# Decode attention with a gated MLP: wq as the moving operand of the query projection, and head selection by a mask on VectorE

## The chip, the cores and the metric

The kernel runs on one core of one Trainium2 chip. The metric is the device time of one execution in microseconds (us). A core has a tensor engine (PE; its weight loads are listed as PEld), a vector engine (DVE), a scalar engine (ACT), POOL, and SP, which here issues the loads. Sixteen DMA engines serve the core.

## The reference, cut to what matters

```python
# B=2 sequences, one new token each; H=32 heads, Sk=16384 cached keys, Dh=128, D=1024, bf16
q      = (x @ wq).reshape(B, 1, H, Dh)                       # wq: 1024 x 4096, 8 MB
scores = einsum(q, k_cache) * Dh**-0.5                       # k_cache: 268 MB
o      = einsum(softmax(scores), v_cache)                    # v_cache: 268 MB
a      = o.reshape(B, 1, H * Dh) @ wo                        # wo: 8 MB
# b = a small MLP of x with w1 .. w4 (19 MB);  result = g * a + (1 - g) * b
```

Every cached byte is used once. The inputs are 572.5 MB.

## The kernel before

The caches are read as 32 tiles (one sequence and two heads each) of 8 MB of K and 8 MB of V. Three buffers of 8 MB rotate: a load is issued when the buffer that it takes has been used up. For each tile, DVE transposes K in 16 pieces, PE multiplies the pieces with the query (`S`), a softmax follows, and PE multiplies with V.

The query projection takes wq as the stationary operand, so that every matmul loads 128x128 weights in order to multiply two columns:

```python
        qps = misc_psum([P, H, B])
        for h in range(H):
            for r in range(KC):
                nc.tensor.matmul(qps[:, h, :], lhsT=wq[:, r, h * Dh : (h + 1) * Dh],
                                 rhs=xT[:, r, :], start=(r == 0), stop=(r == KC - 1))
        nc.vector.tensor_copy(out=qT[:], in_=qps[:])
        # ... 8 matmuls with a 0/1 matrix selv arrange q as the K stage needs it (qsel)
```

The PV product `O` is 128 rows by 4x128 columns, of which each row has one useful quarter. ACT copies all of it to SBUF, and four fp32 matmuls with 0/1 matrices pick the quarters:

```python
        Os = ppool.tile([P, 4, Dh], FP32, tag="PrOs", name="Os")
        nc.scalar.copy(out=Os[:].rearrange("p x d -> p (x d)"), in_=O[:])
        for x in range(4):
            nc.tensor.matmul(oc[:], lhsT=Os[:, x, :], rhs=osel[:, x, :],
                             start=(x == 0), stop=(x == 3))
```

## Time and profile before

| | before |
|---|---|
| median of 6 runs | 1337.32 us (1337.11 to 1337.46) |
| bytes moved, mean rate | 573.34 MB, 429 GB/s |
| DMA queue's packets, share of 16 engines' time | 99.2% |
| PE, DVE, ACT busy | 62%, 53%, 3% |

These lines are from the page of the profile: busy time of each engine (with its share of the span and its instructions), the DMA row of the 40 slices (9 is 90% or more), and the DMA queues (packets, MB, share of 16 engines' span).

```profile
PE 830.0 (62%) x5415; PEld 381.4 (29%) x5415; DVE 709.2 (53%) x863; ACT 45.5 (3%) x100; POOL 14.3 (1%) x45
...
DMA  9999999999999999999999999999999999999997
...
q1 hardware_dynamic: 12664, 572.54, 99.2%
q8 instruction: 42, 0.69, 0.2%
q14 instruction: 14, 0.11, 0.0%
```

DMA is at 9 in every slice but the last. No engine comes near it. The queue q1 carries the kernel's loads. The queues q8 and q14 carry its own instructions.

The costliest groups show busy time and the mean ns of one instruction, then the idle time before them and what ended most of it.

```profile
L308 PE MATMUL S<-T,z 128*128 128x512 bf16 x2048 | 594.0, 423 | 324.7 <-DVE T L300 309.7
...
L300 DVE STREAM_TRANSPOSE T<-Kn 128x1024 f32<-128x1024 f32 x512 | 611.8, 1229 | 264.1 <-DMA Kn<-in_A_k_cache_dram 215.8
...
L360 ACT COPY Os<-O 128x512 f32<-128x512 f32 x32 | 18.7, 585 | 1067.2 <-PE O L352 1067.2
L362 PE MATMUL misc<-osel,Os 128*128 128x2 f32 x256 | 34.5, 257 | 22.2 <-ACT Os L360 22.2
...
L251 PE MATMUL misc<-xT,wt 128*128 128x2 bf16 x256 | 7.1, 165 | 23.3 <-DVE xT L246 20.4
```

DVE's transposes cost 1229 ns each, and 215.8 us of their 264.1 us of idle time end when a K load lands: DVE waits for DMA. The parts that the change touches are L251 (the projection, 7.1 us busy), L360 (the ACT copies, 18.7 us) and L362 (the selection, 34.5 us).

The next lines are the timeline's (start, duration, engine, line, operation), first from the start of the kernel and then around the end of one tile.

```profile
0.74 0.39 SPq L118 DMA_DIRECT2D wt<-in_A_wq_dram  x1
...
23.00 5.98 PE L251 MATMUL misc<-xT,wt 128*128 128x2 bf16 x219 [20.42 <-DVE xT L246]
...
33.04 0.33 SPq L107 DMA_DIRECT2D Vn<-in_A_v_cache_dram  x1
...
33.76 0.29 DVE L269 CAST qsel<-misc 128x128 bf16<-128x128 f32 x1 [0.49 <-PE misc L262]
...
43.63 2.37 DVE L300 STREAM_TRANSPOSE T<-Kn 128x1024 f32<-128x1024 f32 x2 [8.90 <-DMA Kn<-in_A_k_cache_dram]
```

The projection ends at 33.0 us and the query is ready (L269) at 34.05 us, but K0 lands only at 43.6 us. The V load issued at 33.04 us joins a queue with two K loads of 19.3 us each ahead of it, the first of them under way.

```profile
90.60 0.33 SPq L107 DMA_DIRECT2D Vn<-in_A_v_cache_dram  x1
...
91.62 3.68 PE L352 MATMUL O<-Vn,PT 128*32 128x512 bf16 x64
...
95.34 0.33 SPq L96 DMA_DIRECT2D Kn<-in_A_k_cache_dram  x1
95.35 0.58 ACT L360 COPY Os<-O 128x512 f32<-128x512 f32 x1 [26.99 <-PE O L352]
...
95.99 1.05 PE L362 MATMUL misc<-osel,Os 128*128 128x2 f32 x8 [0.69 <-ACT Os L360]
97.08 0.22 DVE L379 SCALAR_TENSOR_TENSOR OT<-misc,g_bc,rinv 128x2 bf16<-128x2 f32 x1 [4.66 <-PE misc L362]
```

The last PV matmul ends at 95.3 us and OT (L379) is written at 97.3 us. The buffer of V is released at the PV matmuls' end, as SP's issue of the next K at 95.34 us shows. The selection comes after that release.

### The profile page before, as it was taken

To read this page: it belongs to the slowest core of one execution; us is meant where nothing else is said; L and a number is where in the kernel's file an instruction comes from. 1 tells how busy PE (TensorE), PEld (TensorE's weight loads), DVE (VectorE), ACT (ScalarE), POOL (GpSimd) and SP (SyncE) were. 2 spreads that over 40 slices of the span, in tenths; PEclk is the share of its full clock that TensorE was granted. 3 is DMA by queue.
4 is the path that set the end of the run, shared out by engine and by line. 5 is a ranking of instruction groups with operands and counts; after the bars stand their busy time and mean duration, and the time that the engine had idled before them with its cause. 6 is when DMAs were issued, how large, how long until landed. Compare 5 with 4: busy or idle time off the path is not lost.

```text
span 1335.5 us, 12650 instructions
## 1 busy us (share of the span) xinstructions
PE 830.0 (62%) x5415; PEld 381.4 (29%) x5415; DVE 709.2 (53%) x863; ACT 45.5 (3%) x100; POOL 14.3 (1%) x45
## 2 busy tenths in 40 slices
PE   2577665677657755555766555577656557765564
PEld 2233222433225322222322222233222223222232
DVE  0666565366651665545666545566655456665530
ACT  0000000000000000000000000000000000000000
POOL 0000000000000000000000000000000000000000
PEclk9988777688776877778887777888777788877775
DMA  9999999999999999999999999999999999999997
GB/s 409 436 437 433 424 440 424 439 437 428 432 434 439 435 426 429 438 432 438 436 433 430 424 440 437 430 433 433 436 440 430 427 432 434 438 435 436 429 419 308
DMA packets 12728, 573.34 MB, mean 429 GB/s; under 512 B 1784, under 2 KB 1792, under 8 KB 2560
## 3 DMA queue, kind: packets, MB, share of 16 engines
q1 hardware_dynamic: 12664, 572.54, 99.2%
q8 instruction: 42, 0.69, 0.2%
q14 instruction: 14, 0.11, 0.0%
q10 hardware_dynamic: 8, 0.00, 0.0%
HBM read 572.53 MB, written 0.00 MB: 429 GB/s over the span
## 4 chain that ended last, share of the span: by engine, by line
PE 27%; DVE 24%; DMA 19%; another core or an unknown queue 14%; issue 13%; ACT 3%; SPq 0%; ACTq 0%; POOL 0%
DVE T L300 20%; PE S L308 14%; DMA Kn<-in_A_k_cache_dram 13%; PE O L352 7%; DMA Vn<-in_A_v_cache_dram 3%; DMA wo<-in_A_wo_dram 3%; PE misc L213 2%; PE misc L362 2%; PE misc L487 2%; ACT Pr L336 1%; DVE PT L340 1%; ACT Os L360 1%; DVE mx L329 1%; DVE mdiag L322 1%
## 5 line engine op out<-in xcount | busy, mean ns | idle before, releaser
L308 PE MATMUL S<-T,z 128*128 128x512 bf16 x2048 | 594.0, 423 | 324.7 <-DVE T L300 309.7
L300 DVE STREAM_TRANSPOSE T<-Kn 128x1024 f32<-128x1024 f32 x512 | 611.8, 1229 | 264.1 <-DMA Kn<-in_A_k_cache_dram 215.8
L308 PEld LDWEIGHTS <-z 128*128 128x128 bf16 x2048 | 217.7, 106 | 695.4 <-issue 532.1
L352 PE MATMUL O<-Vn,PT 128*32 128x512 bf16 x2048 | 121.4, 390 | 5.0 <-DMA Vn<-in_A_v_cache_dram 5.0
L379 DVE SCALAR_TENSOR_TENSOR OT<-misc,g_bc,rinv 128x2 bf16<-128x2 f32 x32 | 7.0, 220 | 159.3 <-PE misc L362 159.3
L352 PEld LDWEIGHTS <-PT 128*32 128x32 bf16 x2048 | 74.1, 140 | 51.1 <-issue 22.2
L213 PE MATMUL misc<-rs,ones_f 128*128 128x2 f32 x64 | 17.9, 349 | 79.1 <-DVE rs L372 79.1
L360 ACT COPY Os<-O 128x512 f32<-128x512 f32 x32 | 18.7, 585 | 1067.2 <-PE O L352 1067.2
L362 PE MATMUL misc<-osel,Os 128*128 128x2 f32 x256 | 34.5, 257 | 22.2 <-ACT Os L360 22.2
L362 PEld LDWEIGHTS misc<-osel,Os 128*128 128x128 f32 x256 | 31.8, 195 | 37.1 <-ACT Os L360 37.1
L319 DVE TENSOR_REDUCE m<-S 128x1 f32<-128x512 f32 x32 | 22.2, 692 | 36.9 <-PE S L308 36.9
L213 PEld LDWEIGHTS misc<-rs,ones_f 128*128 128x128 f32 x64 | 16.1, 313 | 83.9 <-issue 81.2
L340 DVE STREAM_TRANSPOSE PT<-Pr 128x512 bf16<-128x512 bf16 x32 | 22.7, 711 | 28.7 <-ACT Pr L336 28.7
L336 ACT ACTIVATE Pr<-S,nb 128x512 bf16<-128x512 f32 x32 | 22.0, 687 | 125.0 <-DVE nb L331 122.0
L213 PE MATMUL misc<-mdiag,ones_f 128*128 128x128 f32 x64 | 15.6, 326 | 16.9 <-DVE mdiag L322 16.9
L487 PEld LDWEIGHTS <-wt 128*128 128x128 bf16 x352 | 22.3, 167 | 9.8 <-DMA wt<-in_B_w_dram 8.5
L329 DVE TENSOR_REDUCE mx<-misc 64x1 f32<-64x64 f32 x64 | 14.2, 222 | 18.9 <-PE misc L213 18.5
L276 POOL TENSOR_TENSOR z<-qsel,own 128x32 bf16<-128x32 bf16 x32 | 10.6, 332 | 1205.3 <-PE S L308 1173.9
L251 PE MATMUL misc<-xT,wt 128*128 128x2 bf16 x256 | 7.1, 165 | 23.3 <-DVE xT L246 20.4
L487 PE MATMUL misc<-xn2T,wt 128*128 128x2 bf16 x224 | 14.4, 202 | 8.3 <-DMA wt<-in_B_w_dram 8.3
L376 DVE RECIPROCAL rinv<-misc 128x2 f32<-128x2 f32 x32 | 5.5, 171 | 22.7 <-PE misc L213 22.7
L576 DVE CAST rows<-out_acc 128x256 bf16<-128x256 f32 x1 | 0.4, 425 | 29.9 <-PE out_acc L393 29.9
(78 smaller groups left out, 100.0 us busy)
## 6 DMA issues: line engine op xcount, KB each, us to landing
Vn<-in_A_v_cache_dram SPq DMA_DIRECT2D x2, 4096.0 KB, 47.4
wt<-in_B_w_dram SPq DMA_DIRECT2D x1, 7168.0 KB
w<-in_B_w_dram SPq DMA_DIRECT2D x4, 1792.0 KB, 33.0
wo<-in_A_wo_dram SPq DMA_DIRECT2D x6, 1024.0 KB, 34.4
wt<-in_B_w_dram SPq DMA_DIRECT2D x2, 2048.0 KB, 37.3
wo<-in_A_wo_dram SPq DMA_DIRECT2D x2, 512.0 KB, 18.6
wo<-in_A_wo_dram SPq DMA_DIRECT2D x4, 256.0 KB, 12.7
Kn<-in_A_k_cache_dram SPq DMA_DIRECT2D x32, 51.9
```

Source lines behind the costliest of these rows:

```text
L213: nc.tensor.matmul(ps[:], lhsT=ones_f[:], rhs=src, start=True, stop=True)
L300: nc.vector.transpose(out=T[:].rearrange("p w j s -> p j w s"), in_=Kw[:, m * CW : (m + 1) * CW].rearrange("p (j w e) -> p j w e", w=2, e=32),
L308: nc.tensor.matmul(S[:], lhsT=z[:, v, NM - 1 - m : NM - 1 - m + P], rhs=Tb[:, v // 2, :, v % 2], start=(m == 0 and v == 0), stop=(m == NM ...
L319: nc.vector.reduce_max(out=m[:], in_=S[:], axis=AX.X)
L322: nc.vector.tensor_scalar(out=mdiag[:], in0=ident_f[:], scalar1=m[:, 0:1], scalar2=None, op0=ALU.mult)
L329: nc.vector.reduce_max(out=mx[pa, :], in_=mall[pa, pa], axis=AX.X)
L336: nc.scalar.activation(out=Pr[:], in_=S[:], func=ACTF.Exp, bias=nb[:], scale=scale, accum_out=rs[:])
L340: nc.vector.transpose(out=PT[:], in_=Pr[:])
L352: nc.tensor.matmul(O[32 * g : 32 * g + 32, :], lhsT=PT[:, m : CJ * 32 : 16], rhs=V[:, j0 : j0 + 4, :], start=(m == 0), stop=(m == NM - 1),)
L360: nc.scalar.copy(out=Os[:].rearrange("p x d -> p (x d)"), in_=O[:])
L362: nc.tensor.matmul(oc[:], lhsT=Os[:, x, :], rhs=osel[:, x, :], start=(x == 0), stop=(x == 3))
L487: nc.tensor.matmul(ps[:, c, :], lhsT=w[:, r, :].rearrange("k (p c) -> k p c", c=C)[:, :, c], rhs=actT[:, r, :], start=(r == 0), stop=(r == ...
```

## The change

Its intent is to take work off PE. The projection swaps its operands: x is stationary and 512 columns of wq stream past it, in four column groups of the array at a time. The Trainium skill, "TensorEngine Tiling (Array Packing)", section When to Use Tiling, names this as the stationary-streaming swap with column tiling. The selection becomes a sum of four masked quarters on DVE and one fp32 matmul. A new `zero` tile also lets PE clear the accumulators.

```diff
     def compute_q():
...
-        qps = misc_psum([P, H, B])
-        for h in range(H):
-            for r in range(KC):
-                nc.tensor.matmul(qps[:, h, :], lhsT=wq[:, r, h * Dh : (h + 1) * Dh], rhs=xT[:, r, :], ...)
+        for t in range(2):
+            ps = misc_psum([P, CW])                      # CW = 512
+            for g in range(4):
+                zero_rows(ps, g, CW)
+            for r in range(KC):
+                for g in range(4):
+                    c0 = (4 * t + g) * CW
+                    nc.tensor.matmul(ps[group(g), :], lhsT=xT[:, r, :], rhs=wq[:, r, c0 : c0 + CW],
+                                     start=False, stop=(r == KC - 1), skip_group_check=True)
+            # here, for each t, two DVE copies into qrow; after the loop 32 small matmuls give qsel
...
-        Os = ppool.tile([P, 4, Dh], FP32, tag="PrOs", name="Os")
-        nc.scalar.copy(out=Os[:].rearrange("p x d -> p (x d)"), in_=O[:])
+        Os = ppool.tile([P, Dh], FP32, tag="PrOs", name="Os")
         for x in range(4):
-            nc.tensor.matmul(oc[:], lhsT=Os[:, x, :], rhs=osel[:, x, :], start=(x == 0), stop=(x == 3))
+            Ox = O[:, x * Dh : (x + 1) * Dh]
+            if x == 0:
+                nc.vector.tensor_scalar(out=Os[:], in0=Ox, scalar1=xmask[:, 0:1], scalar2=None, op0=ALU.mult)
+            else:
+                nc.vector.scalar_tensor_tensor(out=Os[:], in0=Ox, scalar=xmask[:, x : x + 1], in1=Os[:],
+                                               op0=ALU.mult, op1=ALU.add)
+        nc.tensor.matmul(oc[:], lhsT=Os[:], rhs=asel[:], start=True, stop=True)
```

More of the change, by code (lines that the diff above doesn't have):

```diff
@@ L156 @@
     nc.vector.memset(neg_half[:], -0.5)
+    zero = const.tile([P, 1], BF16)
+    nc.vector.memset(zero[:], 0.0)
     ones_f = const.tile([P, P], FP32)
@@ L173 @@
     nc.vector.tensor_scalar(out=kill[:], in0=kill[:], scalar1=-1.0e30, scalar2=None, op0=ALU.mult)
-    osel = const.tile([P, 4, G], FP32)
+    osel = t_tile([P, 4, G], FP32, "osel")
     osel_f = osel[:].rearrange("p x a -> p (x a)")
@@ L181 @@
         )
-    selv = t_tile([P, 4, 4, 32], BF16, "selv")
-    nc.gpsimd.memset(selv[:], 0.0)
-    for v in range(4):
-        nc.gpsimd.affine_select(
-            out=selv[:, v],
-            in_=selv[:, v],
-            compare_op=ALU.not_equal,
-            fill=1.0,
-            base=-(64 * (v // 2) + v % 2),
-            pattern=[[0, 4], [-2, 32]],
-            channel_multiplier=1,
-        )
+    xmask = const.tile([P, 4], FP32)
+    nc.vector.reduce_sum(out=xmask[:], in_=osel[:], axis=AX.X)
+    asel = const.tile([P, G], FP32)
+    nc.vector.reduce_sum(out=asel[:], in_=osel[:].rearrange("p x a -> p a x"), axis=AX.X)
+    pick = const.tile([P, 4, B], BF16)
+    nc.vector.tensor_copy(
+        out=pick[:], in_=ident_f[:].rearrange("p (g w) -> p g w", w=32)[:, :, 0:B]
+    )
     own = small.tile([P, 8], BF16)
@@ L238, in compute_gate, with group, zero_rows @@
         )
-    qT = const.tile([P, H, B], BF16)
     qsel = const.tile([P, NHG, B, 4], BF16)
+    def group(g):
+        return slice(32 * g, 32 * g + B)
+    def zero_rows(ps, g, width):
+        nc.tensor.matmul(
+            ps[32 * g : 32 * g + 32, :],
+            lhsT=perm[:, 0:32],
+            rhs=zero[:].to_broadcast([P, width]),
+            start=True,
+            stop=False,
+            skip_group_check=True,
+        )
     def compute_q():
@@ L247, in compute_q @@
         wq = wt.pop("wq")
-        qps = misc_psum([P, H, B])
-        for h in range(H):
-            for r in range(KC):
-                nc.tensor.matmul(
-                    qps[:, h, :],
-                    lhsT=wq[:, r, h * Dh : (h + 1) * Dh],
-                    rhs=xT[:, r, :],
-                    start=(r == 0),
-                    stop=(r == KC - 1),
+        CW = 512
+        HB = CW // Dh
+        qrow = t_tile([P, 2, HB * 4, 2, 32], BF16, "qrow")
+        for t in range(2):
+            ps = misc_psum([P, CW])
+            for g in range(4):
+                zero_rows(ps, g, CW)
+            for r in range(KC):
+                for g in range(4):
+                    c0 = (4 * t + g) * CW
+                    nc.tensor.matmul(
+                        ps[group(g), :],
+                        lhsT=xT[:, r, :],
+                        rhs=wq[:, r, c0 : c0 + CW],
+                        start=False,
+                        stop=(r == KC - 1),
+                        skip_group_check=True,
+                    )
+            for half in range(2):
+                nc.vector.tensor_copy(
+                    out=qrow[:, t, :, half, :].rearrange("p (hw two) i -> p hw two i", two=2),
+                    in_=ps[:].rearrange("p (hw i two) -> p hw two i", i=32, two=2),
@@ L257, in compute_q @@
                 )
-        nc.vector.tensor_copy(out=qT[:], in_=qps[:])
         qs_ps = misc_psum([P, 4, NHG, B])
-        for v in range(4):
-            for a in range(G):
-                nc.tensor.matmul(
-                    qs_ps[64 * a : 64 * a + 64, v],
-                    lhsT=selv[:, v, 2 * a : 2 * a + 2].rearrange("p a w -> p (a w)"),
-                    rhs=qT[:].rearrange("p (n a) b -> p n a b", a=G)[:, :, a, :],
-                    start=True,
-                    stop=True,
-                )
+        for t in range(2):
+            for hh in range(HB):
+                a, n0 = hh % G, NHG // 2 * t + hh // G
+                for v in range(4):
+                    nc.tensor.matmul(
+                        qs_ps[64 * a : 64 * a + 64, v, n0 : NHG // 2 * (t + 1) : HB // G, :],
+                        lhsT=qrow[:, t, 4 * hh + v].rearrange("p h i -> p (h i)"),
+                        rhs=pick[:],
+                        start=True,
+                        stop=True,
+                    )
@@ L358, in pv_rows @@
                 )
-        Os = ppool.tile([P, 4, Dh], FP32, tag="PrOs", name="Os")
-        nc.scalar.copy(out=Os[:].rearrange("p x d -> p (x d)"), in_=O[:])
+        Os = ppool.tile([P, Dh], FP32, tag="PrOs", name="Os")
         for x in range(4):
-            nc.tensor.matmul(
-                oc[:], lhsT=Os[:, x, :], rhs=osel[:, x, :], start=(x == 0), stop=(x == 3)
-            )
+            Ox = O[:, x * Dh : (x + 1) * Dh]
+            if x == 0:
+                nc.vector.tensor_scalar(
+                    out=Os[:], in0=Ox, scalar1=xmask[:, 0:1], scalar2=None, op0=ALU.mult
+                )
+            else:
+                nc.vector.scalar_tensor_tensor(
+                    out=Os[:],
+                    in0=Ox,
+                    scalar=xmask[:, x : x + 1],
+                    in1=Os[:],
+                    op0=ALU.mult,
+                    op1=ALU.add,
+                )
+        nc.tensor.matmul(oc[:], lhsT=Os[:], rhs=asel[:], start=True, stop=True)
     def pv_stage(i):
@@ L386, in pv_stage @@
         )
-    def group(g):
-        return slice(32 * g, 32 * g + B)
     def add_row_product(actT, w_row, last=False):
@@ L403, in start_out @@
         for g in range(NQ):
-            nc.tensor.matmul(
-                out_acc[32 * g : 32 * g + 32, :],
-                lhsT=perm[:, 0:32],
-                rhs=shT[:, 0, 0:1].to_broadcast([P, QW]),
-                start=True,
-                stop=False,
-                skip_group_check=True,
-            )
+            zero_rows(out_acc, g, QW)
         res = const.tile([P, KC, B], FP32, name="cen")
```

## The prediction

> **What bounds the kernel.** The DMA. The page gives 573.34 MB at a mean of 429 GB/s; in the slices the DMA row is 9 everywhere but the last, and the queue's own share is 99.2% of 16 engines' span, against PE 62% and DVE 53%. The packet records say how: 8192 packets of 64 KB, nearly all 2.418 us, back to back: about 27 GB/s on each of 16. The Trainium skill, "DMA: Bandwidth & Descriptors", section Specifications, states a fabric ceiling of 435 GB/s; the slices (424 to 440) agree.  The transposes' own idle time ends mostly with "DMA Kn" (215.8 of 264.1 us).
>
> Loads are early: in the timeline V0 is issued at 33.0 us, and K0 and K1 alone keep the queue full until about 63 us; the next V issue (90.6 us) comes about 11 us before the K load ahead of it can land (estimate, 19.3 us per 8 MB). So an engine has some 10 us of slack before the queue runs dry.
>
> **What the change does.**
> - Query projection: 256 matmuls with 256 weight loads (timeline: 22.6 to 33.0 us, with a 2.9 us hole) become 8 zeroing and 64 moving matmuls of 512 columns. Four-column-group matmuls of PV took 3.68 us per 64, so about 4 us; plus two pairs of PSUM copies (about 0.5 us each, estimate from the 0.42 us cast of 256 columns) and 32 small selection matmuls, about 2 us. q should be ready 2 to 4 us sooner, near 30 to 32 us. But K0 lands at 43.6 us; worth nothing.
> - PV head selection: per tile, ACT copy 0.58 us + 8 fp32 passes 1.05 us go; four dependent DVE operations on 128x128 come (about 0.25 us each, from mdiag's 0.28 us) with 2 passes, about 0.35 us. From the last PV matmul to OT (1.95 us) stays within 0.5 us. It lies after the PV matmuls have released V, so no load moves. DVE gains about 30 us of busy time in all. The last tile's selection ends at 1301.4 us, while w4 and wo still come: nothing there either.
> - Instructions: PE loses 160 pairs in q and 192 in PV, about 704 instructions. The page's "instruction" queue has 42 packets, 0.69 MB, on the same engines. The Trainium skill, "Runtime: NRT & Kernel Launch", section Instruction fetch mechanics, says blocks of 16 KiB, 256 instructions: 42 x 256 = 10752 agrees with PE's 10830 records. The records show each fetch delaying its engine by about 1.4 us (0.93 us, and the following packet 0.5 us longer), and they fall on 8 of the 16 engines in turn: 5 each, 6 on two. The last to finish, one with 6, sets the end. With about 39 fetches the maximum is 5: 0.6 us (gap to the next engine) to 1.4 us saved.
>
> **Prediction.** 1336.6 us, 80% range 1335.2 to 1338.0. Faster by over 2%: 1%; within 2%: 98%; slower: 1%.
>
> **Right, if:** the DMA row stays at 9 and 429 to 430 GB/s; the first transpose still starts at 43.6 us although q is ready sooner; PE busy falls by over 30 us with no change of span; instruction packets fall to 39 or 40; ACT loses its 32 copies of O, DVE rises to about 740 us.
>
> **Wrong, if:** DVE's four operations hold the next transposes so long that a V or K issue comes after the queue is empty (then DMA dips below 9); if q gets later than 43.6 us.

## The result, and the profile after

The changed kernel takes 1337.43 us (median of 6 runs, 1337.31 to 1337.8), against 1337.32 us before: no change. The ratio is 1.0001, with a 95% interval of 0.9988 to 1.0014. Here and below, a ratio is the mean time of one kernel's runs over that of the other's of the same rounds, so it is not quite the ratio of the medians quoted.

The same page lines, after:

```profile
PE 795.9 (60%) x5000; PEld 355.3 (27%) x5063; DVE 757.1 (57%) x998; ACT 26.8 (2%) x68; POOL 12.9 (1%) x40
...
DMA  9999999999999999999999999999999999999997
...
q1 hardware_dynamic: 12664, 572.54, 99.2%
q8 instruction: 40, 0.66, 0.2%
q14 instruction: 14, 0.11, 0.0%
```

By the page, PE lost 34 us of busy time; ACT lost 19 us and DVE gained 48 us. The DMA row did not move, and neither did the time. About a third of PE's 34 us is not real: this trace lacks 63 matmul records (5000 beside 5063 weight loads), all in the group S of the K stage, which the change does not touch and which falls from 594.0 to 582.1 us (next listing). Where no record is missing, as in the pair e6 and e7 below, PE loses 20.8 us. Instruction packets on q8 fell from 42 to 40, and those on q14 stayed at 14.

The groups that answer to those of before:

```profile
L333 PE MATMUL S<-T,z 128*128 128x512 bf16 x1985 | 582.1, 421 | 334.3 <-DVE T L325 312.2
...
L325 DVE STREAM_TRANSPOSE T<-Kn 128x1024 f32<-128x1024 f32 x512 | 612.5, 1230 | 261.2 <-DMA Kn<-in_A_k_cache_dram 209.6
...
L388 DVE TENSOR_SCALAR Os<-O,xmask 128x128 f32<-128x128 f32 x32 | 11.2, 350 | 101.2 <-PE O L377 101.2
...
L392 DVE SCALAR_TENSOR_TENSOR Os<-O,xmask,Os 128x128 f32<-128x128 f32 x96 | 33.7, 351 | 3.4
...
L400 PE MATMUL misc<-asel,Os 128*128 128x2 f32 x64 | 12.4, 264 | 51.0 <-DVE Os L392 51.0
...
L269 PE MATMUL misc<-wt,xT 128*2 128x512 bf16 x64 | 5.8, 540 | 19.7 <-DVE xT L257 19.7
```

The 32 ACT copies and 256 selection passes of before are now 128 DVE operations of 0.35 us and 64 passes. The timeline at the start, and around the end of the same tile:

```profile
2.21 1.04 PE L247 MATMUL misc<-zero,perm 128*32 128x512 bf16 x8 [2.21 <-DVE perm L151]
...
23.18 5.77 PE L269 MATMUL misc<-wt,xT 128*2 128x512 bf16 x64 [19.70 <-DVE xT L257]
...
26.81 1.29 DVE L278 CAST qrow<-misc 128x512 bf16<-128x512 f32 x2 [3.24 <-PE misc L269]
...
28.99 0.33 SPq L107 DMA_DIRECT2D Vn<-in_A_v_cache_dram  x1
...
30.83 0.29 DVE L294 CAST qsel<-misc 128x128 bf16<-128x128 f32 x1 [0.54 <-PE misc L287]
...
43.63 2.37 DVE L325 STREAM_TRANSPOSE T<-Kn 128x1024 f32<-128x1024 f32 x2 [12.37 <-DMA Kn<-in_A_k_cache_dram]
```

The projection's last matmul ends at 28.95 us instead of 33.0, V0 is issued 4.05 us sooner, and the query is ready at 31.1 us, 2.9 us sooner. The first transpose starts at 43.63 us, exactly as before. The gain turns into waiting for K0.

```profile
90.67 0.33 SPq L107 DMA_DIRECT2D Vn<-in_A_v_cache_dram  x1
...
91.69 3.68 PE L377 MATMUL O<-Vn,PT 128*32 128x512 bf16 x64
...
95.41 0.33 SPq L96 DMA_DIRECT2D Kn<-in_A_k_cache_dram  x1
95.42 0.35 DVE L388 TENSOR_SCALAR Os<-O,xmask 128x128 f32<-128x128 f32 x1 [2.94 <-PE O L377]
95.81 1.12 DVE L392 SCALAR_TENSOR_TENSOR Os<-O,xmask,Os 128x128 f32<-128x128 f32 x3
...
97.08 0.35 PE L400 MATMUL misc<-asel,Os 128*128 128x2 f32 x2 [1.71 <-DVE Os L392]
97.47 0.22 DVE L415 SCALAR_TENSOR_TENSOR OT<-misc,g_bc,rinv 128x2 bf16<-128x2 f32 x1 [0.54 <-PE misc L400]
```

From the last PV matmul to OT it is now 2.3 us (95.4 to 97.7) instead of 2.0. This too lies after the next K issue (95.41 us) and is paid out of waiting time: the transposes' idle time that ends with a K load is 209.6 us instead of 215.8.

### The sixteen DMA engines, one by one

A "mean share" hides that the 16 engines do not end together. Each engine ends its part of a load with a 4-byte completion write, and the trace keeps those packets. So for each load one can list how far each engine is behind the first. This is the kernel before, three loads in a row (us of the first engine's completion from the span's start, then the lag of all 16 in ns, sorted):

```
 1014.8     0  66 144 465 546 562 710 | 5665 5669 5683 5763 5793 5800 5855 6026 | 6744
 1034.1     0  66 144 465 546 561 710 | 5665 5668 5683 5763 5793 5800 5854 6026 | 6744
 1053.5     0  66 144 465 546 561 709 | 5665 5668 5762 5793 5800 5854 6026 7096 | 7592
```

Between the second and the third row the records hold one 8 KB packet on q14 and one 16 KB packet on q8. One lag rises by 0.85 us (6744 to 7592), another by 1.41 us (5683 to 7096); the others do not move at all. Each engine streams its own sixteenth of every load (64 KB packets of 2.418 us, 27 GB/s), one packet after the other. An instruction fetch takes time from it, and the engine never makes that time good, because it never idles.

There are three classes: seven engines with no regular fetches, eight that share PE's 16 KB fetches in turn, and one that gets an 8 KB fetch every 128 DVE records. In the kernel before these 8 KB fetches come when DVE has begun 68, 191, 323, 451, 580, 709, 839, 965, 1090, 1219 and 1342 of its 1350 records. (Records include waits, which the page does not count as instructions. The other three packets on q14 do not follow this step, and cost engines of the first class 0.5 to 0.6 us each.) The core is done when the last of the 16 is done with wo.

### The profile page after: what moved, and what is told of

Same layout as the page of the kernel before. It is cut to its first block, busy times and chain, and to the rows that moved or that the text cites. A ratio compares the mean times of both kernels' runs of the same rounds, so it can differ in the third digit from the quotient of the medians.

```text
span 1335.9 us, 11948 instructions
## 1 busy us (share of the span) xinstructions
PE 795.9 (60%) x5000; PEld 355.3 (27%) x5063; DVE 757.1 (57%) x998; ACT 26.8 (2%) x68; POOL 12.9 (1%) x40
## 3 DMA queue, kind: packets, MB, share of 16 engines
HBM read 572.53 MB, written 0.00 MB: 429 GB/s over the span
## 4 chain that ended last, share of the span: by engine, by line
PE 26%; DVE 25%; DMA 23%; another core or an unknown queue 12%; issue 11%; ACT 1%; SPq 0%; ACTq 0%; POOL 0%
DVE T L325 19%; PE S L333 15%; DMA Kn<-in_A_k_cache_dram 13%; PE O L377 7%; DMA wt<-in_B_w_dram 4%; DMA Vn<-in_A_v_cache_dram 3%; DMA wo<-in_A_wo_dram 3%; PE misc L212 2%; DVE Os L392 2%; PE misc L513 2%; ACT Pr L361 1%; DVE PT L365 1%; DVE mx L354 1%; PE misc L400 1%
## 5 line engine op out<-in xcount | busy, mean ns | idle before, releaser
L333 PE MATMUL S<-T,z 128*128 128x512 bf16 x1985 | 582.1, 421 | 334.3 <-DVE T L325 312.2
L325 DVE STREAM_TRANSPOSE T<-Kn 128x1024 f32<-128x1024 f32 x512 | 612.5, 1230 | 261.2 <-DMA Kn<-in_A_k_cache_dram 209.6
L333 PEld LDWEIGHTS <-z 128*128 128x128 bf16 x2048 | 210.8, 104 | 692.3 <-issue 529.8
L388 DVE TENSOR_SCALAR Os<-O,xmask 128x128 f32<-128x128 f32 x32 | 11.2, 350 | 101.2 <-PE O L377 101.2
L400 PE MATMUL misc<-asel,Os 128*128 128x2 f32 x64 | 12.4, 264 | 51.0 <-DVE Os L392 51.0
L392 DVE SCALAR_TENSOR_TENSOR Os<-O,xmask,Os 128x128 f32<-128x128 f32 x96 | 33.7, 351 | 3.4
L400 PEld LDWEIGHTS misc<-asel,Os 128*128 128x128 f32 x64 | 9.7, 191 | 65.2 <-DVE Os L392 60.9
L269 PE MATMUL misc<-wt,xT 128*2 128x512 bf16 x64 | 5.8, 540 | 19.7 <-DVE xT L257 19.7
```

The costliest lines, as they stand in the source:

```text
L325: nc.vector.transpose(out=T[:].rearrange("p w j s -> p j w s"), in_=Kw[:, m * CW : (m + 1) * CW].rearrange("p (j w e) -> p j w e", w=2, e=32),
L333: nc.tensor.matmul(S[:], lhsT=z[:, v, NM - 1 - m : NM - 1 - m + P], rhs=Tb[:, v // 2, :, v % 2], start=(m == 0 and v == 0), stop=(m == NM ...
L388: nc.vector.tensor_scalar(out=Os[:], in0=Ox, scalar1=xmask[:, 0:1], scalar2=None, op0=ALU.mult)
L392: nc.vector.scalar_tensor_tensor(out=Os[:], in0=Ox, scalar=xmask[:, x : x + 1], in1=Os[:], op0=ALU.mult, op1=ALU.add,)
L400: nc.tensor.matmul(oc[:], lhsT=Os[:], rhs=asel[:], start=True, stop=True)
```

## The experiments

Three theories are compared. PE-fetch is the prediction's: the engine with most of PE's fetches ends last. DVE-fetch: the engine with DVE's fetches ends last, and the prediction overlooked it. Neutral: fetches do not matter, bytes alone set the end. All results were correct except where a wrong result is stated. Before-medians are from runs beside them on the same chip.

### One half of the change at a time

`e1_q_only` is the changed kernel with the old head selection. `e2_pv_only` is the kernel before with the new one.

```diff
 e1_q_only, against the changed kernel: the Os/oc part of pv_rows is that of the kernel before
 e2_pv_only, against the kernel before: the Os/oc part of pv_rows is that of the changed kernel (plus xmask, asel)
```

> Only the new query projection; the head selection stays as before. All theories: within 1.0 us of the kernel before, because q is ready at about 31 us and K0 lands at 43.6 us either way. Theory DVE-fetch (the DMA engine that carries all of DVE's 8 KB instruction fetches finishes last; 0.85 us for each fetch): DVE's instruction count hardly moves, so 0 to -0.3 us. Theory PE-fetch (the prediction's: the engine with most of PE's 16 KB fetches finishes last): 320 fewer PE instructions, one fetch fewer, 0 to -1.0 us.

> Only the new head selection; the query projection stays as before. Theory DVE-fetch: 132 more DVE instructions are one more 8 KB fetch on the engine that finishes last: +0.3 to +0.9 us. Theory PE-fetch: 384 fewer PE instructions, one or two fetches fewer: 0 to -1.4 us. Theory neutral (fetches do not matter, DMA bytes alone set the end): 0 within 0.3 us.

The medians were 1337.35 us and 1337.42 us against 1337.36 us before (5 runs each; ratios 1.0000 and 1.0000). So two gains and losses do not cancel: each half is worth nothing. For e2 the DVE-fetch theory's stated range (+0.3 to +0.9) was missed. I had assumed one more fetch for 132 more instructions. The records show 11 in both: in the kernel before the eleventh comes 8 records before DVE's end, and with the new selection it comes at record 1337 of 1449, with the twelfth never reached. The number of fetches, not of instructions, is what counts.

### Many DVE instructions, many PE instructions, much DVE time

```diff
 e3_dve_many, in pv_stage of the kernel before, after the scaling of OT:
+        fill = stat.tile([P, G], FP32, name="fill")
+        nc.vector.tensor_copy(out=fill[:], in_=rinv[:])
+        for _ in range(15):
+            nc.vector.tensor_copy(out=fill[:], in_=fill[:])
 e4_pe_many, at the same place:
+        fill = misc_psum([32, G])
+        for _ in range(96):
+            nc.tensor.matmul(fill[:], lhsT=perm[:, 0:32], rhs=OT[:, b, hg * G : (hg + 1) * G], start=True, stop=True)
 e5_dve_long, at the same place:
+        fill = stat.tile([P, G], FP32, name="fill")
+        nc.vector.tensor_copy(out=fill[:], in_=rinv[:])
+        fill2 = stat.tile([P, G], FP32, name="fill2")
+        nc.vector.reduce_sum(out=fill2[:], in_=fill[:].unsqueeze(2).to_broadcast([P, G, 2000]), axis=AX.X)
```

> The kernel before with 16 tiny dependent DVE copies of 128x2 added per tile, 512 in all, in DVE's idle time (about 2 us per tile). Theory DVE-fetch: 4 more fetches of 8 KB on the engine that finishes last, 4 x 0.85 = +3.4 us (2.5 to 4.2). Theory PE-fetch: 0 to +1 us. Theory neutral: 0 within 0.5 us. In the trace: 18 instruction packets of 8 KB instead of 14, and the largest lag of an engine at the last K tile about 11.9 us instead of 8.4.

> The kernel before with 96 tiny matmuls per tile added after the head selection, 6144 PE instructions in all, about 5 us of PE per tile. Theories PE-fetch and DVE-fetch agree that 24 more fetches of 16 KB fall on 8 engines, 3 each, 3 x 1.4 = 4.2 us later for each of them; with PE's engines the last of all already that is +4.2 us, with DVE's engine about 1.2 us behind them now it is +2.5 to +3.5 us. Theory neutral: 0 within 0.5 us. If the time rises by far more than 4.2 us, the added PE time broke the slack of the loads.

> The kernel before with DVE time instead of DVE instructions: two operations per tile, a tiny copy and one reduction over 4000 elements of about 4.2 us (estimate: 1.05 ns an element, from the 0.69 us of 512 elements and its fixed part), in DVE's idle time; 64 more instructions, half a block of 128. Theory DVE-fetch: DVE time is free, 0 to +0.9 us. A rival, that DVE's busy time or its contention with the loads made the 3.8 us of the 512 small copies: those took about 2 to 3 us per tile, so more than that here, +5 us or over.

`e3_dve_many`: 1341.18 us against 1337.36 us, +3.8 us (ratio 1.0028, interval 1.0015 to 1.0042). The page of this run, and the group of the added copies:

```profile
q8 instruction: 42, 0.69, 0.2%
q14 instruction: 18, 0.15, 0.0%
```

```profile
L390 DVE COPY fill<-fill 128x2 f32<-128x2 f32 x480 | 81.5, 170 | 16.1
```

The packets on q14 are 18 instead of 14, as stated, and 480 of the 512 added copies take 81.5 us of DVE (the other 32 take 5.4 us). At the K load that ends near 1247 us the last engine's lag is 12.8 us instead of 8.4 (about 11.9 was stated), while the next engine is at 7.4 (7.3 before). The time is within the DVE-fetch theory's 2.5 to 4.2 us and far above the at most +1 us that the PE-fetch theory allowed.

`e5_dve_long`: 1337.37 us against 1337.32 us, +0.05 us (ratio 1.0000), although its group is this:

```profile
L390 DVE TENSOR_REDUCE fill<-fill 128x2 f32<-128x4000 f32 x32 | 138.2, 4319 | 1.0
```

138.2 us of added DVE time cost nothing, while 87 us of it in 512 instructions cost 3.8 us. So DVE's time is not what the kernel pays for. Its instruction blocks are.

`e4_pe_many`: 1340.90 us against 1337.36 us, +3.5 us (ratio 1.0027, interval 1.0014 to 1.0039):

```profile
q8 instruction: 66, 1.08, 0.3%
q14 instruction: 14, 0.11, 0.0%
```

There are 24 more packets on q8. The eight engines of PE are at 10.1 to 11.9 us of lag at the same load instead of 6.0 to 7.3, and are now last; DVE's engine, at 8.7 us, no longer is. The +3.5 us is the upper edge of what the DVE-fetch theory stated (2.5 to 3.5), and short of the 4.2 us of the PE-fetch theory, in which PE's engines had been last already. The neutral theory falls with e3 and e4.

### Taking fetches away

`e10_before_lean` moves three small operations of the softmax per tile from DVE to POOL in the kernel before. `e9_lean` does so in the changed kernel, and moves the selection and OT's scaling off DVE as well.

```diff
 e10_before_lean (and e9_lean): for mdiag, nb and rs2
-        nc.vector.tensor_scalar(
+        nc.gpsimd.tensor_scalar(
 e9_lean, besides, in pv_rows:
-        (four masked DVE operations on O)
+        Oc = ppool.tile([P, 4, Dh], FP32, tag="PrOs", name="Oc")
+        nc.scalar.copy(out=Oc[:].rearrange("p x d -> p (x d)"), in_=O[:])
+        nc.gpsimd.tensor_tensor(out=Oc[:], in0=Oc[:], in1=xmask[:].unsqueeze(2).to_broadcast([P, 4, Dh]), op=ALU.mult)
+        for n in (2, 1):
+            nc.gpsimd.tensor_tensor(out=Oc[:, 0:n, :], in0=Oc[:, 0:n, :], in1=Oc[:, n : 2 * n, :], op=ALU.add)
 and in pv_stage:
-        nc.vector.scalar_tensor_tensor(out=OT[...], in0=oc[:], scalar=g_bc[...], in1=rinv[:], ...)
+        ocs = stat.tile([P, G], FP32, name="ocs")
+        nc.scalar.copy(out=ocs[:], in_=oc[:])
+        nc.gpsimd.tensor_tensor(out=ocs[:], in0=ocs[:], in1=rinv[:], op=ALU.mult)
+        nc.gpsimd.tensor_scalar(out=OT[...], in0=ocs[:], scalar1=g_bc[:, b : b + 1], scalar2=None, op0=ALU.mult)
```

> The kernel before with three small operations per tile moved from DVE to POOL, 96 DVE instructions fewer: the 11th DVE fetch (issued at about 1302 us, 8 records before the last of DVE's 1350) falls away. Theory DVE-fetch: DVE's engine ends 0.85 us sooner, but then the PE engine with 6 fetches is the last (lag 9.0 against 9.6 us), so only 0.3 to 0.9 us faster. Together with e1, where PE lost a fetch and DVE did not (-0.01 us), and e9, where both lose, this is the maximum of two terms. Theory neutral: 0 within 0.3 us.

> The changed kernel with DVE relieved of 8 instructions per tile: O goes to SBUF by one ACT copy, the mask and the sums run on POOL, and so do the product with the running maximum, the exponent's bias, the row sum's mask and the scaling of OT. About 256 DVE instructions fewer: 9 fetches of 8 KB instead of 11 on the engine that finishes last. Theory DVE-fetch: that engine ends 1.7 us sooner than in the changed kernel (lag 8.2 instead of 9.9 us), the PE engines have 5 fetches each (lag 7.8 us), so 1.0 to 1.8 us faster than the kernel before. Theory neutral: 0 within 0.3 us. If the longer path through ACT and POOL broke the slack of the loads, slower by 2 us or more.

`e10_before_lean`: 1336.63 us against 1337.31 us, -0.7 us, as the DVE-fetch theory stated. `e9_lean`: 1336.38 us against 1337.31 us, -0.9 us, a little short of its stated range. The runs of both do not overlap with those of before (1337.17 to 1337.57): e10 has 1336.46 to 1336.86 and e9 has 1336.28 to 1336.85. The 95% intervals of the ratios, 0.9982 to 1.0007 and 0.9980 to 1.0007, are wider than this spread and include 1, so by that measure alone neither is proved faster. Lines of the page of e10, and then of e9:

```profile
PE 819.3 (61%) x5352; PEld 382.7 (29%) x5415; DVE 693.1 (52%) x767; ACT 45.6 (3%) x100; POOL 51.7 (4%) x141
...
q14 instruction: 14, 0.11, 0.0%
```

```profile
PE 804.2 (60%) x5000; PEld 360.2 (27%) x5063; DVE 688.7 (52%) x742; ACT 50.7 (4%) x132; POOL 135.6 (10%) x296
...
q8 instruction: 40, 0.66, 0.2%
q14 instruction: 16, 0.13, 0.0%
```

In e10 q14 still holds 14 packets: by the step of 128 records 10 of them are DVE's, the last at record 1221 of 1281, and four are not. (In the kernel before, the eleventh starts at 1291 us, not at the 1302 us of the text above.) The shortfall of e9 is a count again: DVE has 1229 records there, and its tenth fetch comes at record 1216, so there are 10 and not the 9 that I expected. POOL now has 296 instructions and is 10% busy, and q14 has 16 packets, of which those that are not DVE's fell on engines of the first class, which end some 6 us before the others.

All of it in one table. The lag columns are at the K load that ends near 1247 us; "last load" is the last completion write of wo, from the span's start. Both are of the profiled execution alone (1337.80 us in the changed kernel, 1337.28 us in the kernel before), the median is of all runs.

| run | DVE fetches (last one at, us) | PE fetches | lag of DVE's engine, us | largest lag of PE's, us | last load, us | median, us |
|---|---|---|---|---|---|---|
| before | 11 (1291) | 42 | 8.4 | 7.3 | 1331.46 | 1337.32 |
| after | 11 (1202) | 40 | 9.7 | 7.5 | 1331.85 | 1337.43 |
| e1_q_only | 11 (1288) | 41 | 8.4 | 7.4 | 1331.32 | 1337.35 |
| e2_pv_only | 11 (1202) | 41 | 9.4 | 7.5 | 1331.49 | 1337.42 |
| e3_dve_many | 15 (1297) | 42 | 12.8 | 7.4 | 1335.80 | 1341.18 |
| e4_pe_many | 11 (1296) | 66 | 8.7 | 11.9 | 1335.28 | 1340.90 |
| e5_dve_long | 11 (1236) | 42 | 9.6 | 7.4 | 1331.57 | 1337.37 |
| e10_before_lean | 10 (1233) | 42 | 8.7 | 7.3 | 1330.81 | 1336.63 |
| e9_lean | 10 (1277) | 40 | 7.7 | 7.5 | 1330.49 | 1336.38 |

How to read it: where DVE's last fetch comes after 1247 us, add 0.85 us to its engine's lag. Before then has 9.3, after 9.7, e1 9.2, e2 9.4, e3 13.6, e5 9.6, e10 8.7 and e9 8.5. The last load follows these numbers within about 0.3 us, at 1322.0 to 1322.2 us plus the lag (before 1331.46 - 9.3 = 1322.2; e3 1335.80 - 13.6 = 1322.2; e9 1330.49 - 8.5 = 1322.0). PE's engines can get one fetch more after 1247 us, too: with 42 fetches two of the eight have a sixth, so at most 7.3 + 1.4 = 8.7 us, as much as DVE's engine has in e10, which fits that e10 gained no more. In e4 PE's engines set the end: 1335.28 us is 1322.0 us plus 11.9 + 1.4. Which packet belongs to which engine is inferred from these lags and from the step of 128 records. The records themselves carry no engine number.

### With the loads out of the way

Both kernels were cut so that a load brings a quarter of its columns and the engines use that quarter four times. Their outputs are wrong, which doesn't matter for the times.

```diff
-            out=t[:].rearrange("p (j d) -> p j d", d=Dh), in_=cache_rows(A_k_cache, i)
+            out=tk[:, 0 : NJ // 4, :], in_=cache_rows(A_k_cache, i)[:, 0 : NJ // 4, :]      # V likewise
-                in_=Kw[:, m * CW : (m + 1) * CW]...
+                in_=Kw[:, (m % 4) * CW : (m % 4 + 1) * CW]...
-                j0 = m * CJ + 4 * g
+                j0 = (m % 4) * CJ + 4 * g
```

> Wrong result on purpose: each K and V load brings a quarter of its columns, and the engines use that quarter four times over, so that the engines and not the loads limit. The kernel before so cut: 32 tiles of about 31 us (26.5 us of K stage and 5 us from its end to the next transposes, as the first tiles show), 950 to 1060 us.

> The changed kernel cut the same way (wrong result on purpose). With the loads out of the way the change shows its own worth: q is ready 3 us sooner, worth 0 to 3 us once; the selection, from the last PV matmul to OT, is 0.3 us longer (2.27 against 1.96 us in the tile at 95 us), +5 to +12 us over 32 tiles if it lies on the engines' chain. So the changed kernel slower than the kernel before by 2 to 12 us; if the selection is hidden here too, 0 to 3 us faster.

They took 867.21 us (866.91 to 867.72) and 869.39 us (867.95 to 870.5). My 950 to 1060 us was too long. The granted clock was 0.96 here instead of 0.80, and stages of neighbouring tiles can overlap more than in the tiles I had summed; the two were not separated. Busy time and the DMA row of the two, before first:

```profile
PE 779.7 (90%) x5415; PEld 335.4 (39%) x5415; DVE 706.0 (82%) x863; ACT 45.6 (5%) x100; POOL 14.3 (2%) x45
...
DMA  9724433662349524444443333344444443333497
```

```profile
PE 758.9 (88%) x5063; PEld 312.6 (36%) x5063; DVE 736.8 (85%) x998; ACT 26.8 (3%) x68; POOL 12.8 (1%) x40
...
DMA  9724433652439514444443433444444443333497
```

DMA is idle for more than half of most slices here, and PE's busy share is 90 and 88%. Even so, the change is worth +2.2 us in 867 by the medians, or +0.25%, and the spread of the changed kernel's runs (2.6 us) is as large as that: its two runs at a granted clock of 0.96 took 868.0 and 868.4 us, the two at 0.952 took 870.3 and 870.5 us. So the stated +2 to +12 us is met at its lower edge at most, and no gain shows on the engines either. In the page's chain of waits, PE's share falls from 75% to 60% and DVE's rises from 15% to 31%: the work on the chain has changed hands. What this pair settles is the size of the spare time: the engines need some 870 us, at the higher clock of 0.96, for what the loads take 1335 us to bring.

### Which engines are which: a probe that went wrong

The idea was to give the lagging engines fewer bytes. For that I wanted to know which engines take part in a load of few partitions.

```diff
+        if i == NT - 4:                      # one V load of 32
+            p0 = 0
+            for n in (112, 8, 4, 2, 1, 1):   # e11_v_halves: for p0 in (0, 64), 64 partitions each
+                nc.sync.dma_start(out=tv[p0 : p0 + n], in_=src[p0 : p0 + n])
+                p0 += n
```

> The kernel before with the V load of tile 28 cut by partitions into 112, 8, 4, 2, 1 and 1, to see which engines take part in a load of fewer partitions. If the lowest-numbered engines do, engine 0 gets 4 packets of 64 KB more (+9.7 us), engine 1 two more (+4.8), engines 2 and 3 one more (+2.4), 4 to 7 as many as before, and 8 to 15 one fewer (-2.4). If engines 8 to 15 are those with PE's fetches, the eight that lag by 6 to 7 us lag 2.4 us less afterwards, and a version that moves bytes that way ends sooner; if they are 0 to 7, it is the other way round. Time: 0 to +10 us, by which engine number 0 is.

> The kernel before with the V load of tile 28 cut into two loads of 64 partitions, all columns. In e8 the cut into 112, 8, 4, 2, 1 and 1 partitions made 64 KB packets last 4.9 us instead of 2.4 and cost 40 us. If the cause is that the engines then no longer each write their own 8 partitions but share them, two halves put two engines on each group of 8 partitions: 64 KB packets of about 4.8 us for this load, 38 us instead of 19, so +15 to +22 us. If the cause of e8 was the very small loads (4, 2 and 1 partitions), 0 to +1 us here.

`e8_probe` took 1377.19 us (one look), +40 us, and the lags after it were too mixed to read the numbering from: that stays open. In the packet records the 64 KB packets of that load and of the loads beside it lasted up to 9.1 us instead of 2.418. `e11_v_halves` took 1367.48 us (one look), +30 us against the stated +15 to +22: its 64 KB packets lasted some 4.9 us, twice the usual, for about 50 us. Since two plain halves do it too, the smallest loads are not needed for it. Sharing of partitions between engines is the explanation that I had stated beforehand and it fits the doubling, but no run shows which engine wrote to which partition. And the slowness outlasted the load, which I had not foreseen. The rebalancing was not tried.

## Why the prediction was right or wrong

The time, 1337.43 us, lies in the stated range of 1335.2 to 1338.0, and "within 2%" was right. But the range also held no change at all: the 0.6 to 1.4 us that the prediction expected to gain did not come, and the mechanism that it gave for them was wrong (last point). Point by point:

- **The bound.** Right. DMA stayed at 9 and at 429 GB/s. The Trainium skill, "DMA: Bandwidth & Descriptors", section Specifications, gives a fabric ceiling of 435 GB/s; 37 of the 40 slices, at 424 to 440 GB/s, lie on both sides of it.
- **The query is ready sooner and it is worth nothing.** Right: 2.9 us sooner, first transpose at 43.63 us in both, and e1 alone moved the median by -0.01 us. Two sizes were off: 64 moving matmuls took 5.8 us instead of 4 (the weight loads of the first ten rounds of four matmuls are 0.43 us apart, the last six rounds took about 1.5 us together), and the two pairs of copies took 1.29 us each instead of about 1.
- **The selection.** The stretch from the last PV matmul to OT grew by 0.3 us (allowed: 0.5). DVE's four operations took 0.35 us each instead of 0.25: the size was carried over from mdiag, an operation of the softmax on as many elements, which reads SBUF where these read PSUM (whether that is the reason was not tested). So DVE rose to 757 us, not 740. e2 and e5 show that it costs nothing.
- **"PE busy falls by over 30 us."** The page says 34.1 us, but only because of the missing records; 20.8 us in the pair e6 and e7 and 20.0 us in e2 (the selection alone, 830.0 to 810.0 us) are what the change took off PE.
- **Fetches delay their engine.** Right, and now shown: 1.41 us for 16 KB, 0.85 us for 8 KB, and 24 and 4 added fetches cost 3.5 and 3.8 us. The Trainium skill, "Runtime: NRT & Kernel Launch", section Instruction fetch mechanics, gives blocks of 256 instructions; with 42 packets for PE's 10830 records the trace agrees.
- **"The last to finish, one with 6, sets the end."** This step failed. The last to finish was the engine with DVE's fetches, 9.3 us behind the first in the kernel before. PE's fetches did fall to 40 as predicted, but the engines that this relieved (at most 8.7 us of lag before, 7.5 us after) were not last, so the stated 0.6 to 1.4 us did not arrive: DVE's engine got eleven fetches in both kernels. I had counted the queue of 16 KB packets and passed over q14, because 0.11 MB looked like nothing. On one engine it is eleven delays of 0.85 us. e1 (PE loses a fetch, DVE does not: 0.0 us), e10 (DVE loses one: -0.7 us) and e3 show it from both sides.

## What to carry to other kernels

In this kernel the DMA engines never idle while loads are queued, and there time saved on any other engine was worth nothing, whatever the chain of waits names. In a kernel with such a DMA row, look first for when the next load is issued and how much is queued ahead of it. The end was set here by the slowest of the 16 DMA engines rather than by their mean, and what made one slow was the instruction stream: blocks of instructions cost time where busy time did not. The sum is small (e9, the best version here, gains 0.9 us of 1337), and real gains for this kernel would have to come from fewer bytes (inferred: no run with a correct result had fewer).

## What the Trainium skill lacked or had wrong

- "Runtime: NRT & Kernel Launch", section Instruction fetch mechanics, calls the cost of crossing a block "mostly hidden". In this kernel, which is bound by DMA, each 16 KB fetch delayed one DMA engine by 1.41 us and each 8 KB fetch by 0.85 us; 24 more of PE's made the kernel 3.5 us longer, and 4 more of DVE's 3.8 us.
- The same section gives refills of 16 KiB, 256 instructions. PE's agree (16 KB packets). DVE's came as 8 KB packets, one for every 123 to 132 records in the kernel before.
- The same page does not say which DMA engines carry fetches. Here, by the lags, PE's fell on 8 of 16 in turn, and DVE's on a single one.
- "DMA: Bandwidth & Descriptors", section Where 436 GB/s comes from, says that for HBM to SBUF the limit of about 358 GB/s binds, and then gives a measurement of 425 GB/s. This core read 572.53 MB from HBM at 429 GB/s over the whole span, so the 358 GB/s did not bind here and the measurement is the better guide.
- The same page, section Rules for kernel authors, says of two transfers to disjoint partition halves not to bother, because they serialize. The one look at it here agrees with the advice, and adds a cost that this row does not give: cutting one 8 MB load so doubled the time of its 64 KB packets (some 4.9 instead of 2.418 us), for longer than that load, and cost 30 us.
